# Softmax denominators by accumulating DMAs instead of TensorE products, with a re-planned order and a new last inverse transform, in a fused attention and long-convolution kernel

## The chip, the cores and the metric

One Trainium2 chip, one of its cores. The metric is the device time of one execution in microseconds (us), measured for each execution; medians are quoted. "Faster" or "slower" means a difference of more than 2%.

In the lines of the profile PE is TensorE and PEld its weight loads, DVE is VectorE, ACT ScalarE, POOL GpSimd and SP SyncE; a q behind a name is that engine's sequencer, which issues and waits. L691 is line 691 of the kernel and x8 a count of instructions. The granted clock is the share of its full clock that TensorE was given. An eviction copies a finished product out of the banks that TensorE writes.

## The reference, cut to what matters

```python
# q, k, v: (4, 8, 768, 64) fp32; centroids: (8, 16, 64); d_model = 512
q_assign = argmax(einsum('bhsd,hcd->bhsc', q_n, c_n), -1)      # k_assign alike
mask   = q_assign[:, :, :, None] == k_assign[:, :, None, :]
scores = where(mask, q @ k.T / sqrt(64), -1e9)
attn   = exp(scores - max(scores))
attn   = attn / (sum(attn, -1, keepdims=True) + 1e-9)          # the denominators
x      = (attn @ v), heads side by side: (4, 768, 512)
x1, x2, x3 = split(x @ w_proj)
y      = x1 * irfft(rfft(x2) * rfft(filter_fft)) * x3
out    = y @ w_out
```

## The kernel before

Heads are taken in eight groups of four, each in two half groups of two heads: sixteen half groups. For each, TensorE forms scores, ScalarE takes exponentials into one of five buffers `p`, TensorE multiplies them by v (`pair<-p,vraw`), and VectorE adds the six key blocks of `p` into `acc`. Four partition bands of a product of `acc` with ones then give the denominators. They go through memory to be spread over partitions, inverted on VectorE, and broadcast back for the normalisation. Between half groups the same engines find the clusters of the next group ("routing") and do the convolution of the batch before ("hyena").

Nothing is issued in program order. Each piece of work is an `op` with its engines and their estimated times, a due time, and what it reads and writes; a list scheduler places the ops when the kernel is built. Each engine then runs its own list in that order, and an instruction that waits holds what stands behind it.

```python
def acc(e, t=t):                                   # VectorE: sums of exponentials
    P_ = lambda x: T.p[slots[x]][:, :, :S]
    T.nc.vector.tensor_tensor(T.acc[:], P_(t[0]), P_(t[1]) if len(t) == 2 else T.acc[:], op=Alu.add)
# ... [cut]
def den(e):                                        # TensorE: denominators
    for hp in range(2):
        for ch in range(2):
            z = 2 * hp + ch
            T.nc.tensor.matmul(ap(h)[32 * z:32 * z + 32, :384], T.ones32, T.acc[:, hp, ts(ch, 384)],
                               start=True, stop=True)
op(("PE", .68), den, te + 0.5, r=["acc", "ones"], w=[h], alloc=h, kind="den")
op(EV384, total, te + 1.5, r=[h], w=["den"], free=[h])     # eviction, ScalarE or VectorE
if not last:                                       # through memory: den -> dd -> dn -> dr -> rb
    op(("SP", .6), lambda e: T.nc.sync.dma_start(T.dd[os], T.den[0:128:32]), te + 2, ...)
    op(("SP", .6), lambda e: T.nc.sync.dma_start(T.dn, T.dd[os].rearrange("z (a b) -> (z a) b", b=12)), te + 4, ...)
    op(("DVE", .3), lambda e: T.nc.vector.reciprocal(T.dn, T.dn), te + 6, r=[], w=["dn"])
    # ... dr <- dn, rb <- dr (broadcast), then on VectorE xT = (osb + eps) * rb   [cut]
# ... [cut] hyena of a batch: the inverse transform, four times
def I(e, dt=dt, hh=hh):
    for e_ in (1, 0):
        for cs in range(2):
            for n in range(2):
                columns(bk(hh, e_)[:, 192 * cs:192 * cs + 192], T.y[:, 2 if n else e_, cs, ts(dt, 128)],
                        T.inv[:, e_, cs, n], n == 0, n == 1)
# then on VectorE sd = bank +- od (twice), yy = sd +- sd folded (twice), y2 = yy * x3
```

The softmax here doesn't subtract the row's maximum and nothing guards it: scores larger than these inputs give would overflow.

Of the kernel before, what the change touches and what calls it, by code (L numbers as in the profile page):

```python
# [33 lines left out]
NU = 4  # L34
HELD = 4
# [14 lines left out]
class Op:  # L50
    __slots__ = ("eng", "fn", "due", "deps", "outs", "left", "ready", "end", "start", "on",
                 "alloc", "free", "lat", "lock", "byts", "seq", "kind", "whole")
# [18 lines left out]
class Plan:  # L71
# [6 lines left out]
    def op(self, eng, fn, due, r=(), w=(), alloc=None, free=(), lock=False, byts=0, after=(), kind=None):  # L78
# [5 lines left out]
        deps = set(after)  # L84
# [20 lines left out]
    def place(self, free0, banks_for, switch=0.1, wait=0.1, rate=215e3, bonus=2.592, margin=0.43, shape=0.33):  # L105
# [4 lines left out]
        st = SimpleNamespace(pool=0.0, dve=0.0, bw=0.0, last=None, kind=None, score=0, o=0, tail=0,  # L110
# [4 lines left out]
        def enqueue(o):  # L115
            o.ready = max([d.end + (0.06 if o.eng.keys().isdisjoint((d.on,)) or d.byts else 0.0)
                           for d in o.deps] or [0.0])
            for e in o.eng:
                ready[e].append(o)
# [13 lines left out]
        def done(o, e, t, d, end):  # L133
            o.start, o.on = t, e
            o.end = end + AFTER.get(e, 0.0)
            if o.byts:
                s = max(o.end + 1.3, st.bw)
                st.bw = s + o.byts / rate
                o.end = st.bw + 0.6
# [21 lines left out]
        while any(ready.values()):  # L161
            best = None
            for e, lst in ready.items():
# [14 lines left out]
                if not cand:  # L178
# [4 lines left out]
                    + (shape if e == "PE" and array(c[1], st.last) != st.last else 0.0)  # L183
                    + (c[0] - t0) * 20, c[1].seq))
# [45 lines left out]
def build(T):  # L230
# [3 lines left out]
    T0 = 9.454  # L234
    TAU1 = 3.31
    TAU2 = 3.644
    NE = 28

# [35 lines left out]
    def load_qk(n, pr, j, due, after=()):  # L274
        s = qslot[n, pr, j] = len(loads) % NQK
        loads.append(1)

        return [op({"SP": .8, "ACT": .8} if n == 0 else ("SP", .8), lambda e, hp=hp: dma(e)(
            T.qkraw[s][:, :, hp], (T.q, T.k)[j][n // 2, 4 * (n % 2) + 2 * pr + hp].rearrange(
                "(p t) d -> p t d", t=NT)), due, w=[("qkraw", s, hp)], byts=196e3, kind="load", after=after)  # L280
            for hp in range(2)]
# [156 lines left out]
    def masks(n, prs, due):  # L438
        aset = n % 2
        out = []  # L440
        for pr in prs:
            for hp in range(2):
                for j in (1, 0):
                    r0 = 32 * (2 * pr + j) + 16 * hp
                    out.append(op(("SP", .6), lambda e, pr=pr, hp=hp, j=j, r0=r0: dma(e)(
                        T.augs[aset][pr][hp][j][64 - 64 * hp:80 - 64 * hp], T.ohT[r0:r0 + 16]), due + .3 * hp,
                        r=[("ohT", pr), ("zero", aset, pr, j)], w=[("augm", aset, pr, hp, j)], byts=25e3))
        return out

    def first_masks(pr):  # L450
# [35 lines left out]
        if pr == 0:  # L486
            for j in (1, 0):
# [8 lines left out]
                for hp in range(2):  # L496
                    def put(e, j=j, hp=hp, h2=h2):
                        rs = slice(64 - 64 * hp, 80 - 64 * hp)
                        o, x = T.augs[0][0][hp][j][rs], ap(h2).bitcast(BF16)[rs, :S]
                        if j:  # L500
                            copy(e, o, x)
                        else:
                            V().tensor_scalar(o, x, BIG, -BIG, op0=Alu.mult, op1=Alu.add)
                    got = op({"ACT": .83, "DVE": .68} if j else ("DVE", .68), put, due + 1.2 + .3 * hp, r=[h2, ("zero", 0, 0, j)],
                             w=[("augm", 0, 0, hp, j)], free=[h2])
# [14 lines left out]
    def routing(n):  # L520
        V = lambda: T.nc.vector
        aset, g = n % 2, n % 2
# [3 lines left out]
        for u in range(8):  # L526
# [26 lines left out]
            if ch == 1:  # L553
                for hp in range(2):
                    op({"ACT": .83, "DVE": .5, "POOL": .85} if n < 1 else {"ACT": .83, "DVE": .5}, lambda e, pr=pr, hp=hp, j=j, z=z: copy(
                        e, T.augs[aset][pr][hp][j][64 * hp:64 * hp + 64],
                        T.qkT[z][64 * hp:64 * hp + 64].rearrange("p a b -> p (a b)")), due + 8 if n else due + 6,
                       r=[("qkT", z, 0), ("qkT", z, 1), ("zero", aset, pr, j)], w=[("aug", aset, pr, hp, j)], lock=True)
        if n == 0:
            return got + first_masks(1)  # L560
        b0 = end - 24.593
# [61 lines left out]
    first = [None]  # L623

    def attention(n, pr, sins):
        aset, b, g = n % 2, n // 2, n % 2
# [4 lines left out]
        last = (n, pr) == (NG - 1, 1)  # L631
        ob = Bank("o", 2)
        for sk in range(NT):
# [4 lines left out]
            for u in range(3):  # L638
                h = Bank("score")

                def sc(e, u=u, sk=sk, h=h):
                    c = 0
                    for hp, lo, hi in THIRDS[u]:
                        K = 80 if hp == 0 else 128
                        ag = T.augs[aset][pr][hp]
                        columns(ap(h)[:, c:c + hi - lo], ag[1][:K, ts(sk, 128)], ag[0][:K, lo:hi], True, True)
                        c += hi - lo
                op(("PE", .217), sc, a + .25 * u, r=[(w, aset, pr, hp, j) for w in ("aug", "augm") for j in range(2)
                                                     for hp, _, _ in THIRDS[u]], w=[h], alloc=h, kind="score")
# [24 lines left out]
            todo = {1: [(0, 1)]}.get(sk, [(sk,)] if sk else [])  # L674
            for t in todo:
                def acc(e, t=t):
                    P_ = lambda x: T.p[slots[x]][:, :, :S]
                    T.nc.vector.tensor_tensor(T.acc[:], P_(t[0]), P_(t[1]) if len(t) == 2 else T.acc[:], op=Alu.add)  # L678
                op(("DVE", 1.75), acc, due + .2 - 40 * (last and sk == NT - 1), r=sum(map(PK, t), []),
                   w=["acc"], lock=True)  # L680
        te = A(i0 + NT) + 2.0 - 40.0 * last
        os = kt % 2
        op(("ACT", .83), lambda e: T.nc.scalar.copy(T.osb[os], two(ob)[:, :, :385]), te, r=[ob], w=[("osb", os)],  # L683
           free=[ob])
        h = Bank()

        def den(e):
            for hp in range(2):
                for ch in range(2):
                    z = 2 * hp + ch  # L690
                    T.nc.tensor.matmul(ap(h)[32 * z:32 * z + 32, :384], T.ones32, T.acc[:, hp, ts(ch, 384)],  # L691
                                       start=True, stop=True)
        op(("PE", .68), den, te + 0.5, r=["acc", "ones"], w=[h], alloc=h, kind="den")

        def total(e):
            if e == "ACT":
                T.nc.scalar.activation(T.den, ap(h)[:, :384], Act.Copy, bias=EPS * S)
            else:
                T.nc.vector.tensor_scalar(T.den, ap(h)[:, :384], EPS * S, None, op0=Alu.add)
        op(EV384, total, te + 1.5, r=[h], w=["den"], free=[h])  # L700
# [415 lines left out]
```

## Time and profile before

| | before |
|---|---|
| time, 3 executions | 401.22 us median (399.67 to 401.58) |
| span of the profiled execution | 398.5 us, mean granted TensorE clock 0.992 |
| busy shares | TensorE 95%, VectorE 91%, ScalarE 69%, GpSimd 4% |
| end of the last value product, which ends the attention | 348.8 us |

### The profile page before, as it was taken

Reading aid. Unit: us, or ns where it says so; the run is one execution under the profiler, and the core shown is the slowest. Engines: PE = TensorE matmul, PEld = TensorE weight load, DVE = VectorE, ACT = ScalarE, POOL = GpSimd, SP = SyncE. Lnnn points to the kernel's source line nnn. Section 1 sums busy time; section 2 is a strip of 40 time slices with the busy share of each in tenths; the row PEclk is TensorE's granted clock in tenths of the full one; section 3 lists DMA queues with packets and bytes.
Section 4 is the critical chain, followed back from the end, with each engine's and each line's share of the span. In section 5 each row is a group of like instructions: output and inputs, shape, how many; then the busy total and the mean of one; then the engine's idle time right before and its main releaser. Section 6 shows DMA issues by size and latency. Waiting matters only on the chain.

```text
span 398.5 us, 8781 instructions
## 1 busy us (share of the span) xinstructions
PE 378.5 (95%) x3447; PEld 204.9 (51%) x3447; DVE 360.7 (91%) x485; ACT 274.6 (69%) x518; POOL 16.8 (4%) x55
## 2 busy tenths in 40 slices
PE   3988999999999999999999999999999999999963
PEld 3543555554445555665455555665455465555731
DVE  8889896996899999999799999999889999989981
ACT  5897889798865886768764886778865667532412
POOL 8700000000000000000000000000000000000000
PEclk9999999999999999999999999999999999999988
DMA  9939959154512415134712414111512010100304
GB/s 177 227 62 226 199 118 234 41 130 116 138 42 61 120 26 114 33 86 141 225 42 58 123 26 103 44 56 52 189 43 60 2 42 3 43 2 7 153 2 159
DMA packets 67233, 37.09 MB, mean 93 GB/s; under 512 B 56700, under 2 KB 62328, under 8 KB 67192
## 3 DMA queue, kind: packets, MB, share of 16 engines
q1 hardware_dynamic: 62856, 33.62, 33.5%
q0 software_dynamic: 1056, 2.10, 2.9%
q10 hardware_dynamic: 3280, 0.82, 1.2%
q8 instruction: 27, 0.44, 0.5%
q14 instruction: 14, 0.11, 0.1%
HBM read 30.66 MB, written 6.48 MB: 93 GB/s over the span
## 4 chain that ended last, share of the span: by engine, by line
PE 89%; ACT 4%; DMA 2%; DVE 2%; issue 1%; ACTq 0%; SPq 0%
PE bank L68 34%; PE pair L668 31%; PE bank L770 5%; PE bank L539 4%; PE bank L691 3%; PE bank L66 3%; PE bank L567 3%; ACT p L657 2%; PE bank L434 2%; DMA qkraw<-in_k_dram 1%; PE bank L580 1%; PE bank L549 1%; DMA aug<-ohT 1%; ACT p L654 1%; PE bank L460 1%
## 5 line engine op out<-in xcount | busy, mean ns | idle before, releaser
L668 PE MATMUL pair<-p,vraw 128*64 128x385 f32 x768 | 141.8, 490 | 1.0 <-ACT qkT L244 1.0
L657 ACT ACTIVATE p<-bank 128x512 f32<-128x512 f32 x192 | 113.3, 608 | 30.2 <-PE bank L68 26.7
L678 DVE TENSOR_TENSOR acc<-p,acc 128x1536 f32<-128x1536 f32 x64 | 112.2, 1754 | 6.6 <-ACT p L657 4.5
L668 PEld LDWEIGHTS pair<-p,vraw 128*64 128x64 f32 x768 | 52.2, 136 | 48.4 <-issue 40.9
L68 PE MATMUL bank<-aug,aug 128*64 128x256 bf16 (+3 forms) x654 | 69.9, 326 | 0.5 <-DMA aug<-ohT 0.4
L654 ACT ACTIVATE p<-bank 128x512 f32<-128x512 f32 x96 | 58.2, 606 | 3.0 <-PE bank L68 2.9
L68 PEld LDWEIGHTS <-aug 128*64 128x64 bf16 (+1 forms) x654 | 36.0, 110 | 31.5 <-issue 16.1
L68 PE MATMUL bank<-xT,wpj 128*64 128x384 bf16 x480 | 48.0, 326 | 0.0
L68 PEld LDWEIGHTS <-wpj 128*64 128x64 bf16 x480 | 26.9, 109 | 20.8 <-issue 11.5
L244 ACT COPY qkT<-bank 128x384 f32<-128x384 f32 x55 | 25.1, 485 | 16.1 <-PE bank L539 6.2
L678 DVE TENSOR_TENSOR acc<-p,p 128x1536 f32<-128x1536 f32 x16 | 28.0, 1750 | 4.4 <-ACT p L657 4.4
L244 ACT CAST aug<-qkT 64x768 bf16<-64x768 f32 x36 | 30.0, 833 | 2.5 <-DVE qkT L246 1.7
L68 PEld LDWEIGHTS <-y 128*64 128x64 bf16 x416 | 21.0, 112 | 15.6 <-issue 4.7
L794 DVE TENSOR_TENSOR tm<-bank,hm 128x512 f32<-128x512 f32 x44 | 27.9, 681 | 0.0
L68 PE MATMUL bank<-wout,y 128*64 128x512 bf16 x160 | 21.2, 405 | 3.5 <-DVE y L860 3.5
L770 PE MATMUL bank<-wpj,xT 128*64 128x512 bf16 x192 | 22.8, 379 | 0.0
L244 ACT COPY ob<-bank 128x512 f32<-128x512 f32 x18 | 10.3, 586 | 16.3 <-PE bank L68 15.4
L683 ACT COPY osb<-pair 128x770 f32<-128x770 f32 x16 | 12.8, 802 | 12.0 <-PE pair L668 11.7
L539 PE MATMUL bank<-ident,qkraw 128*128 128x128 f32 x144 | 20.0, 280 | 0.0
L539 PEld LDWEIGHTS bank<-ident,qkraw 128*128 128x128 f32 x144 | 15.5, 140 | 8.5 <-issue 4.1
L783 DVE TENSOR_TENSOR uv<-tm,bank 128x512 bf16<-128x512 f32 x24 | 15.3, 682 | 4.0 <-PE bank L770 2.1
L770 PEld LDWEIGHTS <-xT 128*64 128x64 bf16 x192 | 10.7, 110 | 10.8 <-issue 3.1
(146 smaller groups left out, 429.2 us busy)
## 6 DMA issues: line engine op xcount, KB each, us to landing
vraw<-in_v_dram SPq DMA_DIRECT2D x16, 384.0 KB
qkraw<-in_q_dram SPq DMA_DIRECT2D x30, 192.0 KB
qkraw<-in_k_dram SPq DMA_DIRECT2D x30, 192.0 KB
rb<-dr SPq DMA_DIRECT2D x30, 192.0 KB
out_dram<-ob SPq DMA_DIRECT2D x11, 512.0 KB
y<-in_moe_filter_fft_dram SPq DMA_DIRECT2D x4, 384.0 KB
wpj<-in_moe_w_proj_dram POOLq DMA_DIRECT2D x1, 1536.0 KB, 12.3
aug<-ohT SPq DMA_DIRECT2D x60, 24.0 KB
```

The lines of the kernel that those rows point to most:

```text
L66: return T.nc.tensor.matmul(out, lhsT, rhs, start=start, stop=stop)
L68: T.nc.tensor.matmul(out[64 * i:64 * i + 64], lhsT[:, 64 * i:64 * i + 64], rhs, start=start, stop=stop)
L244: T.nc.scalar.copy(out, in_)
L539: T.nc.tensor.transpose(bank(h.ids[i // 3])[:, ts(i % 3, 128)], raw(s, i), T.ident)
L654: T.nc.scalar.activation(o, ap(h).rearrange("p (a b) -> p a b", a=2), Act.Exp, scale=0.125)
L657: T.nc.scalar.activation(flat(s)[:, lo:lo + 512], ap(h), Act.Exp, scale=0.125)
L668: T.nc.tensor.matmul(o[64 * hp:64 * hp + 64, ch, :385], T.vraw[vs][:, hp, sk * D:(sk + 1) * D], T.p[slots[sk]][:, hp, 384 * ch:384 * ch + ...
L678: T.nc.vector.tensor_tensor(T.acc[:], P_(t[0]), P_(t[1]) if len(t) == 2 else T.acc[:], op=Alu.add)
L683: op(("ACT", .83), lambda e: T.nc.scalar.copy(T.osb[os], two(ob)[:, :, :385]), te, r=[ob], w=[("osb", os)], free=[ob])
L770: T.nc.tensor.matmul(ap(h)[64 * i:64 * i + 64], T.xT[xs][:, kt, c:c + 64], T.wpj[:, kt, DM:2 * DM], start=kt == 0, stop=kt == ND - 1)
L783: op(("DVE", .68), lambda e, m=m, e_=e_, o_=o_, h=h: T.nc.vector.tensor_tensor(T.uv2[:, e_, m], T.tm[m % 2][:, 0], ap(h), op=o_), due + 1, ...
L794: op(("DVE", .68), lambda e, i=i, cs=cs, r=r, h=h: T.nc.vector.tensor_tensor(T.tm[r][:, cs], ap(h), hmrow(i, (0, 2, 2, 3)[2 * r + cs]), op ...
```

## The change

Its intent is to take ten of the sixteen denominator products (groups 2 to 6) from TensorE, which was never idle in the middle. Three accumulating DMAs fold `acc` from 128 partitions to 16, the 16 rows go through memory, and VectorE adds them after the gather. The other six half groups keep their products. Around it: two sum buffers, a third output buffer, three sets of score operands in a ring; a scheduler in which the DMA queues share one rate, with re-tuned constants; the projection weights in four loads; and, for the last batch, an inverse transform in which TensorE forms the sums and differences itself.

```diff
@@ attention
-        op(("PE", .68), den, te + 0.5, r=["acc", "ones"], w=[h], alloc=h, kind="den")
+        late = n == NG - 1 or n < FIRST          # FIRST = 2
+        if late:
+            ...                                   # the product as before   [cut]
+        if not last:
+            if late:
+                ...                               # dd and dn as before   [cut]
+            else:
+                rows = 64
+                while rows >= ROWS:               # ROWS = 16
+                    op(("POOL", .8), lambda e, rows=rows: T.nc.gpsimd.dma_start(
+                        flat_()[:rows], flat_()[rows:2 * rows], accum_op=Alu.add), te, r=[], w=[("acc", os)],
+                       byts=rows * 9e3, lat=1.5)
+                    rows //= 2
+                op(("SP", .6), lambda e: T.nc.sync.dma_start(T.dd[os], flat_()[:ROWS]), te + 2, ...)
+                op(("SP", .6), lambda e: T.nc.sync.dma_start(T.dp, T.dd[os].rearrange("r (p b) -> p r b", b=12)), te + 4, ...)
+                def gather(e):
+                    T.nc.vector.tensor_reduce(T.dn, T.dp[:].rearrange("p r b -> p b r"), axis=AX, op=Alu.add)
+                    T.nc.vector.tensor_scalar(T.dn, T.dn, EPS * S, None, op0=Alu.add)
+                op(("DVE", .5), gather, te + 6, r=["dp"], w=["dn"])
@@ scheduler
-    def place(self, ..., bonus=2.592, margin=0.43, shape=0.33):
+    def place(self, ..., bonus=8.964, margin=0.036, shape=2.605):
+                    + (BUSY if e == "DVE" and len(c[1].eng) > 1 else 0.0)      # BUSY = 1.562
-                s = max(o.end + 1.3, st.bw)       # one DMA queue for all
+                s, b = max(o.end + 1.3, st.bw.get(e, 0.0)), o.byts / rate      # one each, sharing the rate
@@ hyena, last batch only
+                if last:
+                    for cs in range(2):
+                        for g in range(2):
+                            for e_ in range(2):
+                                for n in range(2):
+                                    columns(bk(hh, cs)[:, 192 * g:192 * g + 192], T.y[:, 2 if n else e_, cs, ts(dt, 128)],
+                                            T.neg[:, cs, n] if e_ and g else T.inv[:, e_, cs, n], e_ + n == 0, e_ + n == 2)
-            for s_, o_ in ((0, Alu.add), (1, Alu.subtract)):
+            for s_, o_ in ((0, Alu.add), (1, Alu.subtract))[:0 if last else 2]:
... [cut: buffers, due times, score ops tied in sequence, order of attention and routing, four loads of w_proj,
     four y sums of the last batch allowed on GpSimd]
```

## The prediction

> **What bounds the kernel now.** I read the page's busy shares first, then a table of busy time by stretches, then the costliest groups, then two pieces of the TensorE timeline, and last the timeline of the queue that issues the DMAs.
>
> The shares of the page, whose columns are engine, busy us, share of the span and instructions:
>
> ```profile
> PE 378.5 (95%) x3447; PEld 204.9 (51%) x3447; DVE 360.7 (91%) x485; ACT 274.6 (69%) x518; POOL 16.8 (4%) x55
> ```
>
> Two engines are near full, so an average can't say which one sets the pace. The table by stretches (start:end, length, then busy us of PE, PEld, DVE, ACT, POOL, granted clock, DMA share, GB/s) can:
>
> ```profile
> 20.00:30.00 10.00, 8.26 (x49) 4.50 (x48) 8.98 (x13) 9.19 (x20) 0.00 (x0) 1.00 0.34 62
> ...
> 100.00:350.00 250.00, 250.00 (x2328) 134.22 (x2324) 238.02 (x302) 178.77 (x337) 0.00 (x0) 1.00 0.28 74
> ```
>
> From 100 to 350 us TensorE is never idle, at full clock: there the time is the sum of TensorE's instructions, and taking one away shortens the span by its slot. VectorE is at 238 of 250 (95%): it allows a few per cent, no more. ScalarE has 71 us to spare and the DMA engines 72%. The 20 us in which TensorE is idle (398.5 - 378.5) lie at the start (6.1 in the first ten us) and at the end (10.3 of the last 17.5).
>
> The groups concerned (columns: line, engine, operation, names, shapes, count, busy us, mean ns, idle before):
>
> ```profile
> L691 PE MATMUL bank<-acc,ones 128*32 128x384 f32 x128 | 13.6, 498 | 0.0
> ...
> L678 DVE TENSOR_TENSOR acc<-p,acc 128x1536 f32<-128x1536 f32 x64 | 112.2, 1754 | 6.6 <-ACT p L657 4.5
> ...
> L851 DVE TENSOR_TENSOR sd<-bank,od 128x384 f32<-128x384 f32 x28 | 14.2, 546 | 0.2
> ```
>
> The first is the denominators' product: sixteen of them, eight instructions each (fp32 counts twice). The second and its sister (16 of 1750 ns) sum the exponentials; the change leaves all 80. What one denominator costs TensorE is read from starts in the timeline, since marked durations overlap:
>
> ```profile
> 314.31 1.46 PE L668 MATMUL pair<-p,vraw 128*64 128x385 f32 x8
> 315.70 0.85 PE L691 MATMUL bank<-acc,ones 128*32 128x384 f32 x8
> 316.48 0.84 PE L68 MATMUL bank<-aug,aug 80*64 80x512 bf16 x8
> 317.16 1.46 PE L668 MATMUL pair<-p,vraw 128*64 128x385 f32 x8
> 318.46 0.82 PE L68 MATMUL bank<-xT,wpj 128*64 128x384 bf16 x8
> 319.11 0.82 PE L68 MATMUL bank<-aug,aug 80*64 80x512 bf16 x8
> ```
>
> The value product ahead of it takes 315.70 - 314.31 = 1.39 us to the next start; the undisturbed one at 317.16 takes 1.30. The denominator itself takes 0.78, the scores after it 0.68 where an undisturbed group of eight takes 0.65. So one costs 0.78 + 0.09 + 0.03 = 0.90 us, and 0.93 where a value product follows (1.35 against 1.29 over the whole timeline).
>
> The end:
>
> ```profile
> 381.39 0.41 PE L68 MATMUL bank<-wout,y 128*64 128x512 bf16 x2 [0.20 <-DVE y L860]
> 385.06 6.63 PE L68 MATMUL bank<-wout,y 128*64 128x512 bf16 x44 [3.26 <-DVE y L860]
> ```
>
> Here TensorE waits for VectorE: 3.5 us in all. VectorE runs without a gap from 357.4 to 387.5 in its timeline, so the last 30 us are VectorE's.
>
> The denominator's way of one pair through memory, on the sync queue:
>
> ```profile
> 159.60 0.54 SPq L702 DMA_DIRECT2D dd<-den  x1
> 161.27 0.33 SPq L704 DMA_DIRECT2D dn<-dd  x1
> 166.38 5.80 SPq L445 DMA_DIRECT2D aug<-ohT  x8
> 172.28 0.53 SPq L708 DMA_DIRECT2D dr<-dn  x1
> 173.98 1.12 SPq L711 DMA_DIRECT2D rb<-dr  x2
> ```
>
> Some 16 us from sum to broadcast, of which the queue spends nearly six on masks. Only 0.8 us of VectorE waits are for this chain: it has slack.
>
> [...] 0.09 to 0.10 us on the group before and 0.03 to 0.06 on the one after a change of the last number in 128*64, 128*32, 128*128; I count 107 changes, some 16 us at about 0.15. [...] No accumulating DMA runs in the kernel before, so its rate is unmeasured here. [...] the two weight loads land after 12.3 us (3.1 MB read) and 5.7 us (1.05 MB), a line with 2.4 us at zero and 318 GB/s. [...]
>
> **The change part by part.**
>
> *Denominators, groups 2 to 6 (ten of sixteen pairs).* Removed: ten products, 10 x 0.90 to 0.93 = 9.0 to 9.3 us of TensorE, all between 110 and 330 us where it is never idle. Also ten evictions of about 0.49 us, nearly all on ScalarE (14 of 16), which has room. Added: three accumulating DMAs each (64, 32, 16 partitions onto the ones below), a write of 16 rows (98 KB), a gather of 2048 pieces of 48 bytes, and on VectorE a reduction of 192 elements and an add of 12. Estimated from the trace: the reduction 0.35 us[...], the add 0.22 like the 12-element reciprocal, together about 0.5: 10 x 0.5 = 5 us more on VectorE. DMA, estimated: accumulations 2.4 us fixed plus 1 to 2, falling, about 11 us for three;[...] gather 2048/16 packets of 11 ns (the trace's own mean for 48 bytes) plus 2, so 3.5. The chain thus grows from two hops of about 2 us each to some 17 us, off TensorE. The next user of that sum buffer is two pairs later; two buffers and an attention pair of 21.8 us cover it. The normalisation of a batch lands some 13 us later, which the diff meets by starting the hyena work 8 us later and by a third output buffer. Groups 0, 1 and 7 stay as they are, so nothing of this reaches the end.
>
> *The planner.* The penalty on changing the array shape goes from 0.33 to 2.605. Of the 107 changes 20 leave with the ten products (counted above); the 24 input transposes, most of them visited singly, can be paired more often. Ten to twenty fewer changes at 0.15: 1.5 to 3 us. The new penalty of 1.562 on VectorE for work that ScalarE could do moves casts and copies: between 100 and 350 us VectorE has 18.2 us of them at one line. The slack demanded before a TensorE instruction falls from 0.43 to 0.036 us, and here I charge something (below).
>
> *The last batch's inverse transform.* TensorE does sums and differences itself: four groups double, each 0.66 us (16 narrow products, from its starts), so +2.6 us at the end. VectorE drops eight sum/difference operations, 8 x 0.47 start to start = 3.8 us, and up to four bf16 sums of 0.60 go to GpSimd, 2.4 us. VectorE sets the end there: its 30 us fall by about 5; TensorE's 3.5 us of waiting shrink by less, as it has 2.6 us more to do. Net gain 1 to 2 us, and one dependent step (0.5 us) is gone from the last chain.
>
> *Loads.* Weight loads in four pieces, after the same filter load as before; DMA isn't the bound at any point past 60 us. Worth 0 to 0.5 us: only one mask wait (0.43 us near 90 us) is in TensorE's line.
>
> The sum: -9.2 (products) - 2 (changes of shape) - 1.5 (end) = -12.7 us. Against it I put +2.5: VectorE would be at 238 + 5 - 10 (shifted, a guess at half of what can move) = 233 of about 239 us, 97.5%, so late sums will sometimes hold the exponentials' buffers; and the tighter planning leaves small gaps on TensorE. Net -10.2: 401.2 - 10.2 = 391.0 us.
>
> **Rivals.** *VectorE takes over as the bound.* For it: 95% now, five us added, TensorE's load lowered under it. Against it: the planner's penalty and ScalarE's 29% of idle time. If little moved, 243 us of VectorE replace 250 of TensorE and the gain of the middle is some 6 us: about 395. *The long DMA chain turns into a wait.* VectorE runs in order, so a gather that lands late stops the sums behind it; ten stops of 1 us would give back the products' gain: about 400. For it: no measured rate of an accumulation[...]. Against it: slack of a whole pair, idle DMA engines. *The work removed was a filler.* If TensorE waits were hidden behind the products, nothing would be gained, but no wait is there in 250 us; I give it little. *Better packing:* if twice as many shape changes go and no gaps appear, 386.
>
> **Range and chances.** The product's 9 us are the surest; a range of 386 to 396.5 covers the lower end with no gaps and the upper with VectorE as the bound. Two per cent is 393.2, 2.2 us above my figure: faster by over 2% 0.68, within 2% 0.29, slower 0.03.
>
> **What would show it.** In the profile after: the product group L691 at 48 instead of 128 instructions; TensorE's busy sum about 368 to 371; its idle time between 100 and 340 us under 3 us (over 5: the planning or VectorE rival); VectorE's waits for the gathered rows under 2 us in total (over 5: the chain rival); fewer than 80 changes of shape; the double inverse groups at about 1.3 us each; in the last stretch TensorE waiting under 2 us for VectorE's products. The prediction fails if TensorE's busy sum falls as said and the span does not.

The forecast's sum: -9.2 - 2 - 1.5 = -12.7 us, 2.5 held against them, -10.2 in all. The estimate of the way through memory: its some 17 us were about 11 for the accumulations, 3.5 for the gather and the rest for the write. Beside the gather's fixed 2 us, an estimate, the trace of the kernel before has such hops at 1.67 to 1.79 us (from the issue of dd to that of dn, four times between 110 and 185 us), and its 3840 packets of 48 bytes took 10.6 ns in the mean. The 0.35 us for the reduction is an estimate too; reductions of 384 and 768 numbers took 550 and 949 ns there, and a line through both gives 0.35 us at 192. The two small times ahead of the count of 107 are what a change of array shape took on TensorE in the starts of the trace, as in the value product of 1.39 us against 1.30.

## More of the kernel before

```profile
PE 89%; ACT 4%; DMA 2%; DVE 2%; issue 1%; ACTq 0%; SPq 0%
```

VectorE is busy 91% of the time and yet has 2% of the chain: what ended last had hardly ever waited for VectorE. Such a chain says who held the pace, not how much room the others had.

## The result, and the profile after

| | before | after |
|---|---|---|
| time, 4 executions each | 400.53 us (399.67 to 401.58) | 396.10 us (395.66 to 396.19) |
| ratio | | 0.9886, 95% interval 0.9856 to 0.9916: same |
| span of the profiled execution | 398.5 us | 394.4 us |
| last value product ends | 348.8 us | 348.9 us |
| from there to the end | 49.7 us | 45.5 us |

A ratio is the mean time of one kernel's fast runs over the mean of the other's fast runs of the same rounds, so it is not quite the ratio of the medians. The gain is 4.4 us where 10.2 were forecast. And the last value product ends at the same time in both profiles, within 0.1 us: all that shows of the gain is in the end. (The profile after lost about a microsecond to a clock dip near 32 us, which the experiments take out; then the middle gained 1.1 us.) Of the forecast 11.2 us for the middle (9.2 for the products, 2 for changes of shape) about a tenth arrived (8.7 were left after the 2.5 that the prediction held against it).

The page's busy shares of the kernel after:

```profile
PE 374.7 (95%) x3355; PEld 214.7 (54%) x3358; DVE 359.2 (91%) x491; ACT 271.1 (69%) x512; POOL 45.3 (11%) x89
```

TensorE's sum fell by 3.8 us only (378.5 to 374.7). Marked durations overlap (a value product marked 1.46 us had the next start after 1.39), and the same 768 value products are marked with 141.8 us before and 146.4 after. VectorE has not become lighter. Then its chain of the work that ended last:

```profile
PE 67%; DVE 20%; issue 4%; ACT 4%; DMA 2%; SPq 1%; ACTq 0%; POOL 0%; DVEq 0%; POOLq 0%
```

VectorE's share of the chain has gone from 2% to 20%. The two tables of busy time for the 240 us from 100 to 340, first before, then after (columns: start:end, length, then busy us of PE, PEld, DVE, ACT, POOL, granted clock, DMA share, GB/s):

```profile
100.00:340.00 240.00, 240.00 (x2222) 128.77 (x2218) 228.09 (x290) 173.02 (x326) 0.00 (x0) 1.00 0.28 76
```

```profile
100.00:340.00 240.00, 236.93 (x2088) 137.10 (x2088) 230.55 (x307) 171.91 (x322) 24.69 (x31) 1.00 0.61 117
```

TensorE now shows idle time, VectorE has gone from 95.0% to 96.1%, and ScalarE, which was to take work over from VectorE, has become 1.1 us lighter, although 4.9 us of evictions of denominators left it. The GpSimd time in the second line is nearly all the issue of the accumulating DMAs (23.9 of 24.7 us, 30 of them). What the change did to VectorE's list between 100 and 350 us is in the groups by line, before and after:

```profile
L246 DVE CAST aug<-qkT 64x768 bf16<-64x768 f32 x12 | 6.6, 550 | 0.4
L246 DVE COPY qkT<-bank 128x384 f32<-128x384 f32 x11 | 5.7, 543 | 0.6 <-PE bank L539 0.5
...
L246 DVE COPY x<-bank 128x384 f32<-128x384 f32 x6 | 3.3, 548 | 0.0
```

```profile
L260 DVE CAST aug<-qkT 64x768 bf16<-64x768 f32 x16 | 8.7, 554 | 0.2
...
L743 DVE TENSOR_REDUCE dn<-dp 128x12 f32<-128x192 f32 x10 | 4.9, 486 | 0.0
...
L260 DVE COPY qkT<-bank 128x384 f32<-128x384 f32 x7 | 3.7, 544 | 0.0
...
L744 DVE TENSOR_SCALAR dn<-dn 128x12 f32<-128x12 f32 x10 | 1.7, 174 | 0.3
L260 DVE COPY x<-bank 128x384 f32<-128x384 f32 x3 | 1.6, 531 | 0.0
```

Copies did leave VectorE (11 to 7 of qkT, 6 to 3 of x), but casts came (12 to 16). With the small rest of that line, casts and copies were 18.3 us before and are 17.6 us after: 0.7 us moved. The gather added 4.9 + 1.7 = 6.6 us. The table shows only 2.5 of the 5.9 us between them: the new order placed some other work of VectorE outside the stretch.

The new DMA steps, from the list of issues (names, queue, operation, count, KB each, median us from issue to landing):

```profile
acc<-acc POOLq DMA_DIRECT2D x10, 384.0 KB, 4.7
acc<-acc POOLq DMA_DIRECT2D x10, 192.0 KB, 3.9
...
acc<-acc POOLq DMA_DIRECT2D x10, 96.0 KB, 3.6
dd<-acc SPq DMA_DIRECT2D x10, 96.0 KB, 3.4
dp<-dd SPq DMA_DIRECT2D x10, 96.0 KB, 2.9
```

That is 18.5 us in all, near the 17 estimated, and no wait of VectorE for the gathered rows (dp) is listed in this profile. At the far end of the chain there is one, for the broadcast reciprocals of one of the ten pairs, at 254 us (what waited, for what: total us, times, longest):

```profile
DVE xT L779 <- DMA rb<-dr: 1.8, 1, 1.8
```

Before, this wait was 0.3 us between 100 and 345 us. So the long chain was hidden but for these 1.8 us. The end, on TensorE's timeline:

```profile
380.39 0.66 PE L72 MATMUL bank<-inv,y 128*64 128x192 bf16 x12
380.89 0.33 PE L72 MATMUL bank<-qkraw,y 128*64 128x192 bf16 x4
...
383.66 0.82 PE L72 MATMUL bank<-xT,wpj 128*64 128x384 bf16 x8
384.31 4.70 PE L72 MATMUL bank<-wout,y 128*64 128x512 bf16 x42
```

The first two lines are half of one doubled inverse group. The next half, not shown, starts at 381.05, so a half takes 0.66 us and the group 1.32 us, as forecast. The last one is the output product: 42 instructions in 4.70 us, 112 ns each, without a wait. Before, 44 of them took 6.63 us, 151 ns each, after a wait of 3.26 us. In the kernel before the granted clock was 0.50 from 385.5 to 388.9 us, just behind that wait; in the same stretch of the kernel after it was 1.00. So the wait went together with a second cost, a slow stretch of TensorE.

### The profile page after: what moved, and what is told of

Read it like the earlier page. It is cut to its first block, busy times and chain, and to the rows that moved or that the text cites. A ratio compares the mean times of both kernels' runs of the same rounds, so it can differ in the third digit from the quotient of the medians.

```text
span 394.4 us, 8641 instructions
## 1 busy us (share of the span) xinstructions
PE 374.7 (95%) x3355; PEld 214.7 (54%) x3358; DVE 359.2 (91%) x491; ACT 271.1 (69%) x512; POOL 45.3 (11%) x89
## 4 chain that ended last, share of the span: by engine, by line
PE 67%; DVE 20%; issue 4%; ACT 4%; DMA 2%; SPq 1%; ACTq 0%; POOL 0%; DVEq 0%; POOLq 0%
PE bank L72 25%; PE pair L685 25%; DVE acc L699 6%; PE bank L811 4%; PE bank L70 4%; PE bank L553 3%; PE bank L582 2%; DMA aug<-ohT 2%; ACT p L674 2%; DVE aug L260 1%; PE bank L448 1%; PE bank L713 1%; ACT p L671 1%; DVE tm L835 1%; DVE uv L824 1%
## 5 line engine op out<-in xcount | busy, mean ns | idle before, releaser
L685 PE MATMUL pair<-p,vraw 128*64 128x385 f32 x768 | 146.4, 493 | 1.3 <-DVE inv L260 1.3
L685 PEld LDWEIGHTS pair<-p,vraw 128*64 128x64 f32 x768 | 57.9, 137 | 51.0 <-issue 39.9
L72 PE MATMUL bank<-aug,aug 80*64 80x512 bf16 (+3 forms) x544 | 72.7, 328 | 0.6 <-DMA aug<-ohT 0.6
L733 POOL DMA_DIRECT2D acc<-acc x30 | 23.9, 795 | 247.0 <-DVE acc L699 93.0
L72 PEld LDWEIGHTS <-aug 80*64 80x64 bf16 (+1 forms) x544 | 35.1, 110 | 29.2 <-issue 20.5
L258 ACT COPY qkT<-bank 128x384 f32<-128x384 f32 x60 | 27.7, 501 | 12.7 <-PE bank L72 9.2
L72 PEld LDWEIGHTS <-y 128*64 128x64 bf16 x480 | 25.1, 110 | 10.6 <-issue 2.6
L70 PE MATMUL bank<-aug,aug 80*128 80x512 bf16 (+3 forms) x111 | 25.8, 321 | 3.2 <-DVE x L875 0.8
L258 ACT CAST aug<-qkT 64x768 bf16<-64x768 f32 x30 | 24.9, 830 | 0.5
L703 ACT COPY osb<-pair 128x770 f32<-128x770 f32 x16 | 13.0, 812 | 11.4 <-PE pair L685 11.2
L260 DVE CAST aug<-qkT 64x768 bf16<-64x768 f32 x31 | 18.1, 589 | 0.4
```

What stands on the lines that cost most here:

```text
L70: return T.nc.tensor.matmul(out, lhsT, rhs, start=start, stop=stop)
L72: T.nc.tensor.matmul(out[64 * i:64 * i + 64], lhsT[:, 64 * i:64 * i + 64], rhs, start=start, stop=stop)
L258: T.nc.scalar.copy(out, in_)
L260: (T.nc.vector if e == "DVE" else T.nc.gpsimd).tensor_copy(out, in_)
L685: T.nc.tensor.matmul(o[64 * hp:64 * hp + 64, ch, :385], T.vraw[vs][:, hp, sk * D:(sk + 1) * D], T.p[slots[sk]][:, hp, 384 * ch:384 * ch + ...
L733: op(("POOL", .8), lambda e, rows=rows: T.nc.gpsimd.dma_start(flat_()[:rows], flat_()[rows:2 * rows], accum_op=Alu.add), te, r=[], w=[("ac ...
```

## The experiments

Two theories were put against each other. **Theory V**: in the middle VectorE is so full that it takes over the pace as soon as TensorE is relieved, and the 6.6 us added to it undo the gain. **Theory T**: TensorE still sets the pace, and the new order with its small slack (margin 0.036) leaves gaps on TensorE that eat the gain.

The instruments. All cut kernels keep the instruction order of the kernel they come from; only sizes change or instructions are left out. Besides the time I read three parts off each profile: until the 73rd exponential starts (about 91 us), the **middle** from there to the end of the last value product, and the **end**. The granted clock of the middle was 1.00 in every profile in which it was read; for e12 there is only the page, with nine tenths or more in every slice of the middle. The split matters because the granted clock dips to half (0.51) for 3.4 us near 32 us (some 6.8 us in e2 and e12, an estimate from their slices), in some executions and not in others. The kernel after had one there in its profile, the kernel before none:

```profile
32.20:35.60 3.40, 3.40 (x20) 0.99 (x20) 1.72 (x2) 2.66 (x5) 0.00 (x0) 0.51 1.06 221
```

```profile
32.20:35.60 3.40, 3.40 (x30) 1.14 (x28) 3.32 (x5) 3.16 (x6) 0.00 (x0) 1.00 1.08 252
```

So executions differ by a microsecond or two through dips, while the middle repeats: 256.5 and 256.6 us in two profiles of the kernel after, 257.4 to 257.6 in kernels that leave the middle of before as it was.

| run | made of | TensorE, VectorE | median us | ratio to before (95%) | middle us | end us |
|---|---|---|---|---|---|---|
| before | | | 400.53 | 1 | 257.6 | 49.7 |
| after | | | 396.10 | 0.9886 (0.9856 to 0.9916) | 256.5 | 45.5 |
| e5 | after again | | 395.29 | 0.9862 (0.9837 to 0.9887) | 256.6 | 45.5 |
| e1 | before | -6.3, 0 | 398.49 | 0.9933 (0.9912 to 0.9954) | 255.2 | 49.3 |
| e9 | before | 0, -8.0 | 400.79 | 1.0029 (1.0004 to 1.0054) | 257.5 | 49.7 |
| e10 | before | -6.3, -8.0 | 396.40 | 0.9922 (0.9898 to 0.9945) | 252.7 | 49.7 |
| e14 | before | 0, +5.2 | 402.24 | 1.0069 (1.0039 to 1.0100) | 259.1 | 50.7 |
| e15 | before | -6.3, +5.2 | 399.94 | 1.0007 (0.9988 to 1.0027) | 257.5 | 49.6 |
| e7 | after | -6, 0 | 395.69 | 0.9882 (0.9859 to 0.9905) | 256.4 | 45.5 |
| e2 | after | 0, -4.9 | 391.27 | 0.9766 (0.9741 to 0.9790) | 252.1 | 45.3 |
| e11 | after | 0, -8.0 | 392.49 | 0.9822 (0.9799 to 0.9846) | 253.4 | 45.5 |
| e13 | after | -6, -4.9 | 390.39 | 0.9767 (0.9745 to 0.9788) | 253.0 | 45.5 |
| e6 | after | 0, -6.6 | 393.24 | 0.9816 (0.9789 to 0.9844) | 253.9 | 45.5 |
| e12 | e6 | 0, -6.6 | 394.54 | 0.9880 (0.9854 to 0.9905) | 254.7 | 46.3 |
| e16 | e12 | 0, -6.6 | 393.98 | 0.9868 (0.9842 to 0.9894) | 255.8 | 45.3 |
| e3 | after | 0, casts away | 408.25 | 1.0180 (1.0156 to 1.0204) | 264.7 | 45.5 |
| e4 | after, replanned | products back | 416.38 | 1.0388 (1.0361 to 1.0416) | 260.3 | 60.7 |
| e8 | before, new end | | 397.22 | 0.9911 (0.9885 to 0.9937) | 257.4 | 46.4 |

The third column is the work changed, in us. TensorE's figures are estimates from the slots in the trace (0.63 us for one denominators' product of e1: its slot of 0.78 less about 0.15 for the change of shape); VectorE's are from the durations in the traces; for e12 and e16 it counts against the kernel after. By the 2% rule e2 and e13 are faster than before and e4 is slower; e3, e6 and e11 are unclear, as their intervals cross 2%; all the others are the same.

### e1, e7: relieve TensorE alone

```diff
# e1, on before (wrong on purpose): the ten products stream 8 columns instead of 384
-  matmul(ap(h)[32*z:32*z+32, :384], T.ones32, T.acc[:, hp, ts(ch, 384)], ...)
+  w_ = 8 if 2 <= n <= 6 else 384
+  matmul(ap(h)[32*z:32*z+32, :w_], T.ones32, T.acc[:, hp, ds(384 * ch, w_)], ...)   # evictions read 8 columns 48 times
# e7, on after (wrong on purpose): the similarity products of groups 3 to 7 likewise
-  matmul(..., T.cbd[:, 2 * g + z // 2], T.qkT[z][:, ch], ...)
+  w_ = 8 if n > 2 else 384
+  matmul(..., T.cbd[:, 2 * g + z // 2], T.qkT[z][:, ch, :w_], ...)
```

> The kernel before in its own order of instructions; the ten products of groups 2 to 6 stream 8 columns instead of 384 (the result is wrong on purpose). TensorE loses about 10 x 0.63 = 6.3 us of streaming, the changes of array shape stay, VectorE and ScalarE do the same work as before. If TensorE alone sets the pace of the middle (theory T), the time falls by about 6 us, to 394.3. If VectorE, at 95%, holds it as well (theory V), it falls by 0 to 3 us, to 397.5 or more.

> The changed kernel in its planned order; the similarity products of groups 3 to 7 stream 8 columns instead of 384 (wrong result on purpose), so TensorE loses about 5 x 1.2 = 6 us, VectorE nothing: the counterpart of the run without the reduction. Theory V: 0 to 2 us faster than the changed kernel (394 to 396). Theory T: 5 to 6 us faster (390 to 391).

Measured: e1 398.49 us, its middle 2.4 us shorter for 6.3 us of TensorE; e7 395.69 us, its middle 0.1 to 0.2 us shorter than that of the kernel after, for some 6 us. In the chain of e1, VectorE has already grown from 2% to 10%:

```profile
PE 79%; DVE 10%; ACT 4%; issue 2%; DMA 1%; SPq 1%; POOL 1%; DVEq 0%; POOLq 0%; ACTq 0%
```

And in the 240 us of e7 TensorE's busy time fell by 3.5 us while VectorE's stayed:

```profile
100.00:340.00 240.00, 233.43 (x2086) 136.89 (x2090) 230.42 (x307) 172.46 (x324) 24.63 (x31) 1.00 0.61 116
```

Theory T needs the kernel after to gain from e7, and it didn't. But e7 takes work away at other places than the change did, so it isn't the whole proof; e13 below shows its limit.

### e2, e11: relieve VectorE in the kernel after

```diff
# e2 (wrong on purpose): no row sums
-  T.nc.vector.tensor_reduce(T.dn, T.dp[:].rearrange("p r b -> p b r"), axis=AX, op=Alu.add)
-  T.nc.vector.tensor_scalar(T.dn, T.dn, EPS * S, None, op0=Alu.add)
+  T.nc.vector.tensor_scalar(T.dn, T.dp[:, 0], 1.0, None, op0=Alu.max)
# e11 (wrong on purpose): the sum of the fourth key block, ten times, over one head of two
+  c = slice(0, 1 if t[0] == 3 and 2 <= n <= 6 else 2)
-  T.nc.vector.tensor_tensor(T.acc[os], P_(t[0]), ...)
+  T.nc.vector.tensor_tensor(T.acc[os][:, c], P_(t[0])[:, c], ...)
```

> The changed kernel in its own order; the ten reductions of the gathered rows (0.49 us each on VectorE, 0.42 to 0.49 of slot) are left out, one row is taken in their place (wrong result on purpose). VectorE loses 4 to 5 us in the middle, TensorE nothing. Theory V: 2.5 to 4.5 us faster than the changed kernel (391.5 to 393.5). Theory T (small waits from tight planning, VectorE not involved): within 1 us of 396.

> The kernel after with its order unchanged and the same ten additions halved (8 us off VectorE, nothing off TensorE). Wrong on purpose. Theory V: the time falls by 4 to 7 us, to 389 to 392, with the end of the attention products some 5 us earlier. Theory T (the after kernel is held by TensorE's packing): less than 1 us, 395 or more.

Measured: e2 391.27 us, the middle 4.4 us shorter for 4.9 us of VectorE (a little less may be due, as this profile had a longer clock dip at the start, behind which some slack can be won back). e11 392.49 us, the middle 3.1 us shorter for 8.0; that is less than the 4 to 7 us expected, but far from the "less than 1" of theory T. Where on VectorE's list the time is taken matters: not every microsecond stands on the path. One thing more left with the reductions of e2: the wait of 1.8 us for the broadcast reciprocals fell to 0.3 us, while in e11 it stayed (1.9 us). So a part of e2's 4.4 us can be the shorter chain to memory and not VectorE's time; the two are not parted there. The chain of e2, and its stretch:

```profile
PE 90%; ACT 4%; DVE 3%; issue 1%; DMA 1%; ACTq 0%; POOL 0%; SPq 0%; POOLq 0%; DVEq 0%
```

```profile
100.00:340.00 240.00, 239.60 (x2120) 137.84 (x2120) 230.54 (x301) 174.67 (x329) 24.76 (x31) 1.00 0.63 119
```

Without the ten reductions VectorE leaves the chain, and it looks like that of the kernel before. Its busy share stays at 96.1%, as in the kernel after, because the same stretch now holds more of the work. So the share alone does not tell who holds the pace.

### e9, e10, e14, e15: the exchange itself, in the old order

These ask of the kernel before what each side is worth, alone and together, without the new order, the new DMAs or the new end.

```diff
# e9 (wrong on purpose): as e11, on before.   e10: e1 and e9 together.
# e14 (right result): before each reciprocal of groups 2 to 6
+  T.nc.vector.tensor_reduce(T.scr, T.ident[:, :12].unsqueeze(2).to_broadcast([128, 12, 16]), axis=AX, op=Alu.add)
+  T.nc.vector.tensor_scalar(T.scr, T.scr, EPS * S, None, op0=Alu.add)
   T.nc.vector.reciprocal(T.dn, T.dn)
# e15 (wrong on purpose): e1 and e14 together
```

> The kernel before with its order unchanged; in ten half groups (groups 2 to 6) the addition of the fourth block of probabilities to the row sums runs over one head of the pair instead of both, which takes VectorE from 1754 ns to about half of that, ten times: some 8 us off VectorE, nothing off TensorE. Wrong on purpose in the denominators. Theory V (VectorE and TensorE are both full in the middle and bound each other, VectorE 95%): the kernel before gains a little, 1 to 3 us, since TensorE, marked busy without a gap, holds it: about 398 to 400. Theory T (TensorE alone sets the pace of the kernel before): no gain, 400 to 401.

> The kernel before with both cuts: the ten denominator products stream 8 columns (6.3 us off TensorE, alone worth 2.7 us) and the ten additions run over half the columns (8 us off VectorE). Wrong on purpose. Theory V: the two reliefs together give clearly more than the sum of each alone, 5.5 to 8 us: 392.5 to 395. Theory T: VectorE's relief adds nothing to the 2.7 us: about 398.

> The kernel before with its order unchanged and, ahead of each of the ten reciprocals of groups 2 to 6, a reduction of 192 numbers per partition and an addition, of the sizes that the change brings, on data that is always there: 6.6 us more for VectorE, nothing else. Right result. Theory V: the kernel before has VectorE at 95% beside a full TensorE, its relief gave nothing, but its load costs part: 1 to 4 us, 401 to 404 at a like clock. Theory T: VectorE has 12 us of room in the middle, and the load costs less than 1 us.

> The kernel before with its order unchanged, the ten denominator products cut to 8 columns (6.3 us off TensorE; alone worth 2.4 us of the middle) and the ten reductions and additions added to VectorE (6.6 us): the exchange that the change makes, without its transfers and without a new order. Theory V: the exchange is worth nothing, as in the change: the attention products end within 1 us of the kernel before's, later by as much as 2 us. If the new order or the transfers ate the gain of the change: the attention products end some 2 us earlier than in the kernel before, as with the cut alone.

Measured. e9: nothing gained, against the 1 to 3 us expected. The 240 us of it:

```profile
100.00:340.00 240.00, 240.00 (x2222) 128.93 (x2222) 221.45 (x291) 173.04 (x325) 0.00 (x0) 1.00 0.28 76
```

VectorE went from 228 to 221 us and TensorE stayed at 240.00 with the same 2222 instructions. So TensorE alone bounds the kernel before: my theory V had it wrong there, where it made VectorE a bound of equal rank.

e10: the middle is 4.9 us shorter, where the reliefs alone gave 2.4 and 0.1. VectorE's relief is worth nothing while TensorE is full, and 2.5 us once TensorE is relieved. TensorE is then nearly full again:

```profile
100.00:340.00 240.00, 239.45 (x2274) 133.82 (x2274) 224.39 (x295) 174.61 (x331) 0.00 (x0) 1.00 0.28 75
```

The medians alone hide this (0.9922 against 0.9933 for e1), because of clock dips: the timed executions of e10 had a lower mean clock (about 0.989) than those of before in the same rounds (about 0.993). Compared at a granted clock of 0.989, spans are 399.5 to 400.4 us before, 397.0 in e1 and 394.5 to 394.8 in e10.

e14: the middle is 1.5 us longer. The added reduction turned out cheaper than the real one, 348 ns against 486, so 5.2 us were added rather than 6.6 (it reads each value sixteen times over, the real one values 48 bytes apart; no run shows what makes the difference):

```profile
L709 DVE TENSOR_REDUCE scr<-ident 128x12 f32<-128x192 f32 x10 | 3.5, 348 | 0.0
```

e15: 6.3 us taken from TensorE and 5.2 us added to VectorE give 399.94 us, a ratio of 1.0007: nothing, in the time as in the middle (257.5 us). The stretch and the chain of e15:

```profile
100.00:340.00 240.00, 235.77 (x2220) 131.81 (x2220) 230.80 (x310) 172.53 (x325) 0.00 (x0) 1.00 0.28 75
```

```profile
PE 70%; DVE 15%; ACT 4%; issue 4%; DMA 3%; SPq 2%; POOL 1%; ACTq 0%; DVEq 0%
```

VectorE at 230.8 us, TensorE at 235.8, the chain at 70% and 15%: this is the picture of the kernel after (230.6, 236.9, 67% and 20%), made from the kernel before without touching its order. That an exchange of this kind is worth nothing is thereby shown for the old order, at 6.3 us against 5.2 where the change has about 9 against 6.6. The new order and the accumulating DMAs aren't needed to explain the loss; what they add or take by themselves was not measured.

### e13: both reliefs in the kernel after

```diff
# e2 and e7 together (wrong on purpose)
```

> The kernel after with its order unchanged, the ten row reductions left out (4.9 us off VectorE, alone worth 4.4 us of the middle) and the similarity products of groups 3 to 7 cut to 8 columns (6 us off TensorE, alone worth nothing). Wrong on purpose. Theory V: with VectorE relieved TensorE begins to count, so the two together give more than 4.4 us, 5 to 7 us less than the kernel after: 388.5 to 390.5 at a like clock. If TensorE's relief is worth nothing even then: 391, as without the reductions alone.

Measured: 390.39 us, a ratio of 0.9767 against 0.9766 of e2; the middle 3.5 us shorter than in the kernel after, against 4.4 in e2. TensorE's relief adds nothing even with VectorE relieved, which I did not expect. Up to 256 us e13 stood slightly better than e2, by 0.5 us from the 73rd exponential on. Then it lost 1.9 us at a wait that it did not have before, for the mask rows that the sync queue loads:

```profile
PE bank L70 <- DMA aug<-ohT: 1.9, 1, 1.9
```

So this relief of TensorE runs into the next thing, and e7's "no gain" can't by itself tell VectorE's bound from such waits. The case rests on e15, e2 and e10.

### e6, e12, e16: keep the result right and give VectorE its time back

```diff
# e6: the ten row sums on GpSimd, in halves
-  T.nc.vector.tensor_reduce(...); T.nc.vector.tensor_scalar(...)
+  for r in (8, 4, 2):
+      T.nc.gpsimd.tensor_tensor(T.dp[:, :r], T.dp[:, :r], T.dp[:, r:2 * r], op=Alu.add)
+  T.nc.gpsimd.tensor_tensor(T.dn, T.dp[:, 0], T.dp[:, 1], op=Alu.add)
+  T.nc.gpsimd.tensor_scalar(T.dn, T.dn, EPS * S, None, op0=Alu.add)
# e12: e6, and each of the ten reciprocals two VectorE instructions later, with what depends on it
# e16: e12, and each multiplication by the gathered reciprocals three VectorE instructions later
```

> The changed kernel in its planned order, the sum over the 16 gathered rows and the added constant done by GpSimd (five small operations) instead of VectorE; the result is right. VectorE loses 10 x 0.66 us busy, about 5.5 us of slots, as in the run without the reduction, TensorE nothing. Theory V: 3.5 to 5.5 us faster than the changed kernel (391 to 392.5). Theory T: within 1 us of it. [...]

> The kernel after with the ten gather sums on GpSimd, as before (393.2 us), and now each reciprocal moved two VectorE instructions later, with what depends on it, so that VectorE does not wait for GpSimd's sum (four waits, 3.9 us in all, in the earlier run's waits). Right result. Theory V: most of those 3.9 us come back: 390 to 392. If the waits of VectorE only cover time that it would have waited for something else: 393 again.

> The kernel after with the ten gather sums on GpSimd, each reciprocal two VectorE instructions later, and now also each multiplication by the gathered reciprocals three VectorE instructions later, for which VectorE waited 6.1 us in all in the run before it. Right result. Theory V: VectorE neither waits for GpSimd nor for the rows, and it has 6.6 us less to do than in the kernel after: 4 to 5.5 us less than it, 389.5 to 391 at a like clock. If the wait only moves again: 393 to 394.

Measured: e6 393.24 us, the middle 2.6 us shorter than in the kernel after, less than the 3.5 to 5.5 expected. In its waits (engine and line, what it waited for: total us, times, longest):

```profile
DVE dn L749 <- POOL dn L747: 3.9, 4, 1.1
...
DVE xT L782 <- DMA rb<-dr: 1.3, 2, 0.9
```

The reciprocal on VectorE now waits for GpSimd, whose five small instructions take 2.8 us together. VectorE's long sums were not slowed beside them (1751 ns, and 1749 in e5 without them). e12 removed exactly that wait and gained nothing (394.54 us, the middle 0.8 us longer than in e6). Its waits:

```profile
DVE xT L783 <- DMA rb<-dr: 6.1, 3, 3.0
```

The later reciprocals come back later, and VectorE now stands still at the multiplication instead: 1.3 us became 6.1. e16 moved that multiplication too, and that wait is gone, but now TensorE waits for the later multiplications. Between 100 and 345 us:

```profile
PE bank L815 <- DVE xT L783: 1.6, 2, 1.0
```

(VectorE's longest waits in e16, 3.7 us for the filter and 2.6 us for the rows of an early denominator, are at 41 and 56 us, before the middle.) Its middle is 255.8 us, 1.2 us longer than in e12; the wait shown is the largest of TensorE there, and the rest is not traced. Two hand moves in a packed list each moved the wait to another place. The slack of this chain, which the prediction took for granted, is there only for the places in the list that the scheduler gave it. e6 stays the best kernel with a right result: 393.24 us, 1.8% under the kernel before (unclear by the 2% rule) and about 2 us under the kernel after.

### e3, e4: two misses of the means

```diff
# e3: 28 casts of VectorE given to ScalarE when instructions are emitted, order as it was
-  o.fn(o.on)
+  o.fn("ACT" if o.kind == "cast" else o.on)
# e4: all denominators by products again, planned anew by the new scheduler
-FIRST = 2
+FIRST = 8
```

> The changed kernel in its planned order, but the 28 casts of the score operands of groups 1 to 7 that the planner gave to VectorE (0.55 us each) are issued by ScalarE at the same place (0.83 us each). The result is right. VectorE loses about 28 x 0.5 = 14 us, 9 of it between 100 and 350 us; ScalarE gains 21 us where it has 28% idle. Theory V: 4 to 8 us faster than the changed kernel (388 to 392), with the exponentials a little later. Theory T: no change within 1 us, or slower where the exponentials are held.

> The changed kernel with the denominators of all groups by products again, planned anew with the changed planner: the rest of the change (planner's constants, end, loads) without the accumulating DMAs. TensorE has about 9 us more to do, VectorE about 6.5 us less. Theory T: 6 to 9 us slower than the changed kernel (402 to 405). Theory V: 0 to 3 us slower or even faster (394 to 399): what the DMAs took from TensorE they gave to VectorE.

Measured: e3 408.25 us. A cast takes ScalarE 830 ns and now stands in front of exponentials in its list; so VectorE waits for exponentials instead, here between 100 and 350 us:

```profile
DVE acc L699 <- ACT p L674: 13.6, 7, 6.3
```

VectorE's relief can't be judged from this run. It says only that work is not moved to an engine with idle time for nothing: it must be planned in. e4 416.38 us: the end alone grew from 45.5 to 60.7 us, with TensorE waiting for VectorE's sums and products.

```profile
PE bank L72 <- DVE y L839: 6.2, 2, 5.6
...
PE bank L72 <- DVE y L913: 2.7, 3, 1.9
```

The constants were tuned to another set of ops, so a replanned variant tells of the plan as much as of the change. Its middle, 3.8 us longer than in the kernel after, agrees in sign with a worth of the DMA path under the new scheduler, but is no measure of it. That is why all later runs keep the order fixed.

### e8: the new end alone; e5: the kernel after again

```diff
# e8: before, with the last batch's inverse transform of the change (doubled on TensorE, negated table,
#     four y sums allowed on GpSimd); e5: after, unchanged
```

> The kernel before with only the last batch's inverse transform changed (sums by TensorE, four sums offered to GpSimd); TensorE's order is that of before for its first 3800 of 4560 rows, so the middle is the same. The part by itself: 2 to 5 us faster than before (396 to 399) by both theories, the end of attention unmoved. My prediction had 1 to 2 us for it; the changed kernel's end is 4.1 us shorter.

> The changed kernel once more, so that the others of this call can be held against it on one chip, run by run at the same granted clock. Both theories: 395.5 to 397, and the runs differ by 1.7 us or so according to whether a stretch of 3.4 us at half clock near 32 us is there (mean clock about 0.995 with it, 0.998 without).

Measured: e8 397.22 us, ratio 0.9911; its end is 46.4 us against 49.7. The output product, as in the kernel after:

```profile
384.24 0.82 PE L68 MATMUL bank<-xT,wpj 128*64 128x384 bf16 x8
384.89 4.70 PE L68 MATMUL bank<-wout,y 128*64 128x512 bf16 x42
```

So the new end alone is worth 3.3 us, more than the 1 to 2 of the prediction; some 1.7 us of it is that the output product ran at full clock (112 ns an instruction against 151). It is most of what the whole change gains (ratios 0.9911 and 0.9886 or 0.9862). e5 reproduced the kernel after: 395.29 us, middle 256.6, end 45.5.

## Why the prediction was right or wrong

The time, 396.1 us, lies just inside the range of 386 to 396.5, but the gain was 4.4 us where 10.2 were forecast, and the likeliest class, faster by over 2%, did not come. That the range holds is luck: the end brought 2.6 us more than was booked for it, and without that the time would be about 398.7.

**The step that failed** is VectorE's term in the sum: "VectorE would be at 238 + 5 - 10 (shifted, a guess at half of what can move) = 233 of about 239 us". The 10 us that were to move to ScalarE did not: casts and copies at that line went from 18.3 to 17.6 us. The gather was 6.6 us, not 5. (The reduction was estimated at 0.35 us and took 0.49.) So VectorE rose, from 95.0% to 96.1% of the stretch, instead of falling, and the argument on it ("97.5%, so late sums will sometimes hold") priced at 2.5 us what cost about 8: of the products' 9.2 us the middle gained 1.1. The penalty of 1.562 was read as moving work; in the placed order copies went one way and casts the other, and no run parts that penalty from the other new constants.

**The first rival is what happened**, and it was sized wrongly too. It put VectorE's 243 us in place of TensorE's 250 and kept a gain of 6 us in the middle. That supposes VectorE can be packed to 100%. Here the two kernels in which VectorE has the largest part of the chain (the kernel after and e15) stand at 96% of it, with no single listed wait of VectorE over 1.8 us between 100 and 345 us; in the kernel after the listed ones come to 6.9 us, for exponentials, for broadcast rows and for TensorE. The exchange in the old order (e15) gives zero, so a time for VectorE as the bound had to be read at about 96%, and then there was nothing to gain. That the rival's total of about 395 us lies near 396.1 is luck too: its middle was 5 us too good and the end in its sum 2.6 us too small.

**The products' 9.2 us** left TensorE as said: 48 instructions are left of 128, and the evictions went with them.

```profile
L713 PE MATMUL bank<-acc,ones 128*32 128x384 f32 x48 | 5.1, 497 | 0.8 <-ACT od L258 0.5 <-issue 0.2
```

What was wrong was "there the time is the sum of TensorE's instructions". It holds for the kernel before as it stands (e9 shows it), but e1 shows how far: of 6.3 us taken away, 2.4 came out of the middle, though nothing was added to VectorE; relieving VectorE as well (e10) won back 2.5 of the other 3.9, and 1.4 stay unexplained.

**Changes of shape**: I count 88 in the kernel after, 107 before; "fewer than 80" did not come. Of the 107, 20 were to leave with the ten products; 19 left in all. The ten to twenty further ones, booked with 2 us, did not go.

**TensorE's idle time** of 100 to 340 us was 240 - 236.93 = 3.1 us, against "under 3", and its busy sum 374.7 instead of 368 to 371. Both signs looked nearly right or mildly off and said little: the marked time of the same 768 value products rose by 4.6 us. The chain (TensorE 89% to 67%, VectorE 2% to 20%) said it at once.

**The end** was sized at -1.5 and brought -3.3 alone (e8) and -4.1 in the change's profile. The term left out is the slow stretch after the wait, at a granted clock of 0.50: 44 output products at 151 ns instead of 112, some 1.7 us. And "the last 30 us are VectorE's" was too wide: TensorE was busy for 31.00 of the 31 us from 350 to 381.

**The long DMA chain** cost one wait of 1.8 us at its end (2.0 in e5), not the ten of 1 us that the rival feared, and none for the gathered rows: right in the main. Its slack proved small, though, once the reciprocals were moved by hand (e12).

**Left open**: which hand-over through VectorE costs TensorE its time. VectorE's share of the chain is spread over sums, routing steps and hyena sums, and no single wait carries it. Open too is what the new order is worth alone: e4, planned anew, cannot tell. Also open is how much a scheduler that really moved 10 us to ScalarE would gain; e3 could not tell.

## What to carry to other kernels

When two engines stand at 100% and 95%, taking work from the first is worth only the room that the second has in practice (2.4 of 6.3 us in e1), and here there was none left for an exchange (nothing in e15); price a change that moves work between them as an exchange, and read the chain of the work that ended last beside the busy shares. Don't bank a shift of work that a scheduler's penalty only makes likelier: read the placed order. And test such an exchange with the order held fixed, each side alone and both together: relief that is worth nothing alone can be worth 2.5 us behind another.
